# Attention units 4 to 7: from the weight tiles ahead of the first block to pool tiles between its products

## The chip, the cores and the metric

One core of one Trainium2 chip (trn2) runs the whole program. The metric is the device time of one execution in microseconds; the time of before is the median of three runs. In the views PE is TensorE's matmul stream, DVE is VectorE, ACT ScalarE, POOL GpSimd and SP SyncE, which issues all DMAs here.

## The reference

Three stages follow each other. Attention has four batches, eight heads, 576 tokens and a head dimension of 64, in float32; a gated MLP widens 512 to 1536, a second MLP widens 512 to 2048. The weights are float64.

```python
# attention: a mean over groups of four tokens, plus a window of +-3 tokens
q_d = q.reshape(B, H, Sd, 4, D).mean(axis=3)      # k_d, v_d likewise
out_d = softmax(scale * q_d @ k_d.T) @ v_d
out_up = np.repeat(out_d, 4, axis=2)
out_local = softmax(where(|i - j| < 4, scale * q @ k.T, -1e9)) @ v
x = (out_up + out_local)                          # then (2304, 512)
# gated MLP
g = x @ w_gate
x = (g * sigmoid(g) * (x @ w_val)) @ w_out
# second MLP
h = x @ w_in
out = (max(h, 0) + alpha * min(h, 0)) @ w_out2
```

## The kernel before, in words

**Blocks and steps.** The 2304 tokens form eight blocks of 288 (half a batch's sequence). For each block the first MLP runs twelve steps j, each over 128 of the 1536 hidden columns: `m_g` (12 products into g), `m_v` (12 into v) and, one step late, `m_y` (12 into y, which collects over the twelve steps). Float32 accuracy comes from splitting each operand into a high half and a rest: `mm3` makes three products of each (high by high, high by rest, rest by high). So a step is 36 products of 288 columns, a block 432. After g a Tanh on ACT (L512) and a multiplication on DVE (L513) follow, after v another on DVE (L519), then ph (the high half, ACT L522) and pl (the rest, POOL L523), which y needs.

**Weights.** A float64 weight tile of 512 KB (`raw`) is loaded by SP (L104, L106) and split on the chip by `w_split`, three a step (g, v, o). ACT makes a float32 from the upper words (L129). Then there are two forms. With a staging tile in one of three weight slots (`st_slots`: o10, g11, v11) ACT also fetches the top byte (L137) and DVE joins them in one instruction (L139). With a staging tile "st" of the pool, DVE joins them in two (L131, L132). `NEARLY` says from which step on the second form is used. At last ACT makes the high half (L142) and POOL the low half (L143). The split weights stay on the chip for all eight blocks, so loads and splits happen only in the first 143 us.

**Attention units.** A block needs four units of two heads each, unit n = 4 blk + hp, so units 0 to 3 feed block 0, units 4 to 7 block 1. A unit is `a_T` (k and q transposed), `a_QK` (scores on PE, L345 and L349; the mask, the maxima on DVE, the subtraction on POOL L371), `a_EXP` (ACT L388), `a_NRM` (sums on DVE, the scaling on POOL L408, then four transposes on DVE into a block-diagonal tile bd, L419), `a_PT` (transposes on PE, copied to pt) and `a_PV` (second products on PE, L446 and L450, then up on ACT L454, xf on DVE L455, xh on ACT L459, xl on POOL L460). xh and xl are the block's operand. The units of a batch's first half also sum v in groups of four on POOL (`a_vd`, L332 and L333): the tile vd has one buffer, so its next load waits until both instructions have read it. v's windows are copied within HBM by `stage(b)` (1.5 MB a batch) and then loaded as vw.

**Where the units' tiles lie.** With `NPRO = 8` units 0 to 7 work in weight tiles that no weight needs yet. `pslot` gives each tile a slot: the k tile of units 0 to 3 and the vd tile are used again as q and as scratch by units 4 to 7. From unit 8 on, units use single pool tiles (qn, qT, sm, pt, vw, xf). A weight that shares its slot with a unit's tile can be loaded only when that unit is through.

**What sets the order.** The tile framework's scheduler orders each engine's instructions; the code says where a unit stands: units 0 to 7 are written ahead of the products, later units by `at(position, ...)`, with 36 positions a block (three a step) and `run(position)` between `m_g`, `m_v` and `m_y`. Unit 8's scores stand at position 25 (`OFF`), later ones nine apart, second products eleven positions behind the scores. `prep1(j)` splits a step; `gP` holds POOL's part of the first splits back behind a stage of units 0 to 3. SP issues in order, with eight DMA semaphores in turn, so an issue also waits for the DMA eight places earlier.

Of the kernel before, what the change touches and what calls it, by code (L numbers as in the profile page):

```python
# [18 lines left out]

K = dict(kdP=0, qdP=0, dnP=2, ldn=9, lo='asvw0123', NPRO=8, c=5, a1=1, a2=0, OFF=25, oT=3, oE=3, oP=5, oV=11, vd1=2, vd2=1, pre=(1, 1, 0, 0), lo1=0, lo2=1, nst=3, nrm=0, sub=0, nrm1=0, sub1=0, qtA=0, ldw=1, xl1=0, ly=4, l2=3, st2=2, early=1, w2p=1, la=0, bdV=0, sp=9, s2=0, s3=0, gj=7, gs=1, vr=0, kc=0, gD=(0, 0, 0, 0, 0, 0), gP=(0, 2, 8, 8, 0, 0), gA=(0, 0, 0, 0, 0, 0))  # L20


@with_exitstack
def attn_moe_moe2_kernel(
# [13 lines left out]
    nc = tc.nc  # L38
# [18 lines left out]
    SW = LW + SD  # L57
    NBD, NVD, NVW, NSM, NST = 1, 1, 1, 1, 2
    scale = 1.0 / float(D) ** 0.5
# [99 lines left out]
    order = [f"{kind}{j}" for j in range(F1 - 8, F1) for kind in "gvo"]  # L159
    st_slots = order[5 * NP:][:K["nst"]]  # L160
    NEARLY = F1 - 2
    pslot = {(what, n): order[4 * i + n] for i, what in enumerate(("qv", "qs", "kn", "vd", "bd")) for n in range(NP)}
    for n in range(NP):
        pslot["qv", n + NP] = pslot["kn", n]
        pslot["qs", n + NP] = pslot["qs" if K["vr"] else "vd", n]
    NPRO = K["NPRO"]
# [70 lines left out]
    def a_load_w(n):  # L237

        b, half, hp, blk = coords(n)
        if n < NP:  # L240
            pbd[n] = at_(n, [128, 2, NW, 128], "bd")
            (nc.vector if K["bdV"] else nc.gpsimd).memset(pbd[n], 0.0)
# [149 lines left out]
    def a_NRM(n):  # L392
# [23 lines left out]
        d["bd"] = pbd[n % NP] if n < NPRO else bds[n % NBD]  # L416
        for i in range(NS):
# [70 lines left out]
    def gate(n, stage):  # L488

        bb = tc.nc.cur_bb.bb.instructions  # L490
        for key, eng in (("D", nc.vector), ("P", nc.gpsimd), ("A", nc.scalar)):
            gates[key, n, stage] = next(i for i in reversed(bb) if i.engine == eng.engine)

    def prep1(j):
        with ExitStack() as es:
            for key in "DPA":
                g = K["g" + key][j] if j < 6 else 0
                if g and (key, (g - 1) // 2, (g - 1) % 2) in gates:
                    es.enter_context(tc.issue_after(gates[key, (g - 1) // 2, (g - 1) % 2]))
            prep1_(j)  # L500
# [25 lines left out]
    def m_y(blk, j):  # L526
# [5 lines left out]
        if j == F1 - 1:  # L532
            for e in range(KD):
                if blk == NB1 - 1:
                    ys = side2.tile([128, 512], F32, tag="sy", name="sy", bufs=2)[:, :HB]
                elif e % 2:
                    continue
                else:
                    ys = hp_.tile([128, 2, HB], F32, tag="st", name="ys", bufs=NST)
                n = 1 if blk == NB1 - 1 else 2  # L540
                src = Y[e // 2][:, e % 2, :HB] if n == 1 else Y[e // 2][:, :, :HB]
                nc.scalar.copy(out=ys, in_=src)  # L542
                nc.sync.dma_start(
                    out=y1[e * 128:(e + n) * 128, blk * HB:(blk + 1) * HB].rearrange("(e p) t -> p e t", p=128),
                    in_=ys.unsqueeze(1) if n == 1 else ys)

# [83 lines left out]
    if True:  # L630
# [34 lines left out]
        def a_all(n, A):  # L665
# [13 lines left out]
            if K["vd1"] == 3:  # L679
                a_vd(n)  # L680
            a_PV(n, A)

        pc = [0]
# [7 lines left out]
        for n in range(NP):  # L691
            a_all(n, P[n])
        preps(K["pre"][1])
        pstack.close()
        pg2 = ctx.enter_context(tc.tile_pool(name="pg2", bufs=1, space=PSUM))
        GV[0] = pg2.tile([128, 512], F32, name="g")
        GV[1] = pg2.tile([128, 512], F32, name="v")
        for n in range(NP, NPRO):
            a_load(n)
            a_load_w(n)  # L700
        for n in range(NP, NPRO):
            if n == NP + 2:
                preps(K["pre"][2])
            a_all(n, P[n % NP % 3])
        preps(K["pre"][3])
        def load8():
            if B > 1:
                stage(1)
            a_load(NPRO)
            a_load_v(NPRO)  # L710
            a_load_w(NPRO)

        for j in range(4, F1 - 2):
            load1(j)
        with tc.issue_after(wdma[f"o{K['gj']}"]):
            load8()
        for b in range(2, B):
            if K["gs"] == 0:
                stage(b)
        nc.sync.dma_start(out=alpha_sb, in_=alpha.rearrange("(j p) -> p j", p=128))  # L720
# [38 lines left out]
        for i, (blk, j) in enumerate(fts):  # L759
# [9 lines left out]
            if blk == 0:  # L769
                while pc[0] <= min(j + K["early"], F1 - 1):  # L770
                    prep1(pc[0])
                    pc[0] += 1
                    if pc[0] == NEARLY:
                        load1(F1 - 2)
                        load1(F1 - 1)
                        if K["gs"]:
                            with tc.issue_after(wdma[f"o{F1 - 1}"]):
                                for b in range(2, B):
                                    stage(b)
            m_g(blk, j)  # L780
# [64 lines left out]
```

## Time and profile before

| what | before |
| --- | --- |
| median of three runs | 1017.37 us (1016.74 to 1018.96) |
| the profiled execution | 1017.97 us, span 1015.9 us, mean granted clock 0.995 |
| PE busy | 969.7 us (95%) |
| DVE, ACT, POOL busy | 478.9, 306.8, 383.5 us (47%, 30%, 38%) |
| HBM read, written | 67.12 MB, 15.73 MB |

The busy shares say that PE sets the time on the whole. They are means over stages: loads, splits and units 0 to 7 fill the first 150 us, the blocks with PE full follow. The table of stretches below tells them apart; its columns are the stretch, its length, the busy time and (in brackets) the instructions of PE, PEld (weight loads), DVE, ACT and POOL, the granted clock as a share of full speed, the DMA share and GB/s. In a timeline each line is one instruction (or a few alike): start, duration, engine, line, what it writes and reads, and in brackets the idle time ahead of it with what ended it.

### The profile page before, as it was taken

How to read it: one execution, taken by the hardware profiler on the slowest of the kernel's cores; microseconds unless marked ns; L12 is line 12 of the kernel's file. 1: busy time of each engine (PE TensorE's matmuls, PEld its weight loads, DVE VectorE, ACT ScalarE, POOL GpSimd, SP SyncE). 2: the span in 40 equal slices, each digit the busy share in tenths (PEclk: the TensorE clock that was granted, in tenths of full speed). 3: DMA queues.
4: the chain of work that ended last, by engine and by line, in shares of the span. 5: the costliest groups of instructions: out<-in, count | busy, mean ns of one | idle time of the engine just before them, and what ended most of it. 6: DMA issues, size and time to landing. Idle time of an engine off the chain costs nothing.

```text
span 1015.9 us, 19233 instructions
## 1 busy us (share of the span) xinstructions
PE 969.7 (95%) x7760; PEld 865.3 (85%) x7760; DVE 478.9 (47%) x1015; ACT 306.8 (30%) x690; POOL 383.5 (38%) x492
## 2 busy tenths in 40 slices
PE   5489789999999999999999999999999999999998
PEld 4379679999999999999999998888888888888897
DVE  5577864555444555444532769622222322322232
ACT  3869632222221322222323556312111101211111
POOL 5868763234322344222223435624223322322222
PEclk9999899999999999999999999999999999999999
DMA  8998741132111321110103883102000100100010
GB/s 202 290 315 283 184 93 27 35 73 59 38 46 21 76 50 41 40 26 18 43 9 116 282 254 122 42 1 63 22 0 21 52 1 1 42 11 1 0 43 22
DMA packets 135894, 77.81 MB, mean 77 GB/s; under 512 B 97406, under 2 KB 127102, under 8 KB 135038
## 3 DMA queue, kind: packets, MB, share of 16 engines
q1 hardware_dynamic: 135804, 76.58, 27.0%
q8 instruction: 60, 0.98, 0.4%
q14 instruction: 30, 0.25, 0.1%
HBM read 67.12 MB, written 15.73 MB: 82 GB/s over the span
## 4 chain that ended last, share of the span: by engine, by line
PE 82%; SPq 4%; DVE 4%; DMA 3%; POOL 3%; issue 2%; ACT 2%; POOLq 0%; DVEq 0%; ACTq 0%
PE y L610 7%; PE y L612 6%; PE y L611 6%; PE g L473 6%; PE v L474 6%; PE v L473 6%; PE v L475 6%; PE g L474 6%; PE g L475 6%; PE y L473 4%; PE y L475 4%; PE y L474 4%; PE h L473 3%; PE h L475 3%; PE h L474 3%
## 5 line engine op out<-in xcount | busy, mean ns | idle before, releaser
L598 POOL TENSOR_TENSOR gl<-t,gh 128x512 fp32r<-128x512 f32 (+1 forms) x80 | 97.0, 1214 | 250.9 <-ACT gh L597 244.4
L597 ACT CAST gh<-t 128x512 fp32r<-128x512 f32 (+1 forms) x80 | 46.2, 578 | 278.7 <-DVE t L594 239.2
L473 PE MATMUL g<-xh,w 128*128 128x288 f32 x384 | 117.4, 306 | 10.0 <-DVE u L513 4.4
L475 PE MATMUL g<-xh,w 128*128 128x288 f32 x384 | 115.1, 300 | 1.9 <-POOL w L143 1.8
L473 PE MATMUL v<-xh,w 128*128 128x288 f32 x384 | 116.0, 302 | 0.6 <-ACT w L142 0.4
L474 PE MATMUL v<-xl,w 128*128 128x288 f32 x384 | 115.3, 300 | 0.0
L474 PE MATMUL g<-xl,w 128*128 128x288 f32 x384 | 115.0, 300 | 0.0
L474 PE MATMUL y<-pl,w 128*128 128x288 f32 x384 | 113.8, 298 | 1.3 <-POOL pl L523 1.2
L475 PE MATMUL v<-xh,w 128*128 128x288 f32 x384 | 113.8, 296 | 0.6 <-POOL w L143 0.6
L610 PE MATMUL y<-w,gh 128*128 128x512 f32 x288 | 113.2, 393 | 1.0 <-ACT sy L542 1.0
L475 PE MATMUL y<-ph,w 128*128 128x288 f32 x384 | 113.0, 296 | 0.0
L611 PE MATMUL y<-w,gh 128*128 128x512 f32 x288 | 112.8, 392 | 0.0
L612 PE MATMUL y<-w,gl 128*128 128x512 f32 x288 | 112.0, 392 | 0.0
L513 DVE SCALAR_TENSOR_TENSOR u<-u,g 128x288 f32<-128x288 f32 x96 | 43.3, 451 | 144.1 <-ACT u L512 144.1
L473 PE MATMUL y<-ph,w 128*128 128x288 f32 x384 | 111.0, 301 | 0.2 <-ACT ph L522 0.2
L523 POOL TENSOR_TENSOR pl<-u,ph 128x288 fp32r<-128x288 f32 x96 | 79.8, 832 | 59.4 <-ACT ph L522 58.6
L143 POOL TENSOR_TENSOR w<-st,w 128x512 fp32r<-128x512 f32 x52 | 70.2, 1356 | 60.7 <-ACT w L142 60.5
L473 PEld LDWEIGHTS g<-xh,w 128*128 128x128 f32 x384 | 73.5, 191 | 12.9 <-DVE u L513 5.7
L592 DVE TENSOR_SCALAR t<-h,alpha 128x512 f32<-128x512 f32 (+1 forms) x40 | 27.9, 697 | 110.7 <-PE h L475 109.5
L512 ACT ACTIVATE u<-g 128x288 f32<-128x288 f32 x96 | 39.4, 410 | 122.8 <-PE g L475 121.3
L475 PEld LDWEIGHTS g<-xh,w 128*128 128x128 f32 x384 | 73.7, 192 | 2.7 <-POOL w L143 2.4
L473 PEld LDWEIGHTS v<-xh,w 128*128 128x128 f32 x384 | 72.8, 190 | 2.3 <-DVE u L519 1.0
(190 smaller groups left out, 2143.4 us busy)
## 6 DMA issues: line engine op xcount, KB each, us to landing
raw<-in_moe_w_out_dram SPq DMA_DIRECT2D x28, 512.0 KB
raw<-in_moe_w_in_dram SPq DMA_DIRECT2D x16, 512.0 KB
raw<-in_moe_w_gate_dram SPq DMA_DIRECT2D x12, 512.0 KB
raw<-in_moe_w_val_dram SPq DMA_DIRECT2D x12, 512.0 KB
vw<-vwin SPq DMA_DIRECT2D x48, 96.0 KB
out_dram<-os SPq DMA_DIRECT2D x18, 256.0 KB
sy<-y SPq DMA_DIRECT2D x16, 256.0 KB
y<-ys SPq DMA_DIRECT2D x14, 288.0 KB
```

Source lines behind the costliest of these rows:

```text
L143: eng.tensor_sub(w[:, 1], st, f32(w[:, 0]))
L473: nc.tensor.matmul(o, lhi, rhi, start=first, stop=False)
L474: nc.tensor.matmul(o, lhi, rlo, start=False, stop=False)
L475: nc.tensor.matmul(o, llo, rhi, start=False, stop=last)
L512: nc.scalar.activation(out=u, in_=GV[0][:, :HB], func=AF.Tanh, scale=0.5)
L513: nc.vector.scalar_tensor_tensor(out=u, in0=u, scalar=1.0, in1=GV[0][:, :HB], op0=ALU.add, op1=ALU.mult)
L523: nc.gpsimd.tensor_sub(pl, u, f32(ph))
L597: nc.scalar.copy(out=gh[:, :n], in_=t[:, :n])
L598: nc.gpsimd.tensor_sub(gl[:, :n], t[:, :n], f32(gh[:, :n]))
L610: nc.tensor.matmul(o, gh[:, ms], ohi, start=(j == 0), stop=False)
L611: nc.tensor.matmul(o, gh[:, ms], olo, start=False, stop=False)
L612: nc.tensor.matmul(o, gl[:, ms], ohi, start=False, stop=(j == F2 - 1))
```

## The change

Units 4 to 7 are no longer written ahead of the products. `NPRO` is 4: only units 0 to 3 use weight tiles, and units 4 to 7 take pool tiles and positions of their own: scores seven positions apart from position 1 on (`c = 7`), transposes six, second products seven positions behind the scores. Their q and k come by DVE transposes, not PE transposes. Unit 8 starts at position 30 instead of 25. The slots of units 0 to 3 are dealt out anew: k and vd tiles in the slots of steps 4 and 5 first. `NEARLY` goes from 10 to 8, so that the splits of steps 8 to 11 use the two-step form on DVE (twelve splits, not six), and `st` and the y copies have three buffers. Splits 1 to 3 are held behind unit 3 on DVE, POOL and ACT, not on POOL alone. The copy of y out of PSUM at a block's end is four copies and four DMAs of 288 columns, not two of 576. The windows of batch 1 are copied behind o of step 9, those of batches 2 and 3 at position 36 behind g and v of step 11. Lines of after stand three lines higher from 146 on, one line higher from about 500.

```diff
-K = dict(... NPRO=8, c=5, a1=1, a2=0, OFF=25, ... gj=7, ... gP=(0, 2, 8, 8, 0, 0), ...)
+K = dict(... NPRO=4, c=7, a1=1, a2=0, OFF=30, ... gj=9, ...)
-    NBD, NVD, NVW, NSM, NST = 1, 1, 1, 1, 2
+    NBD, NVD, NVW, NSM, NST = 1, 1, 1, 1, 3
-    NEARLY = F1 - 2
-    pslot = {... enumerate(("qv", "qs", "kn", "vd", "bd")) for n in range(NP)}
-    for n in range(NP):
-        pslot["qv", n + NP] = pslot["kn", n]
-        pslot["qs", n + NP] = pslot["qs" if K["vr"] else "vd", n]
+    NEARLY = F1 - 4
+    pslot = {... enumerate(("kn", "vd", "qv", "bd", "qs")) for n in range(NP)}
+    behind = {1: (NP - 1, 1), 2: (NP - 1, 2), 3: (NP - 1, 2)}
     def prep1(j):
         with ExitStack() as es:
-            for key in "DPA":
-                g = K["g" + key][j] if j < 6 else 0
-                if g and (key, (g - 1) // 2, (g - 1) % 2) in gates:
-                    es.enter_context(tc.issue_after(gates[key, (g - 1) // 2, (g - 1) % 2]))
+            if j in behind:
+                for key in "DPA":
+                    es.enter_context(tc.issue_after(gates[(key, *behind[j])]))
             prep1_(j)
@@ m_y
-                    ys = hp_.tile([128, 2, HB], F32, tag="st", name="ys", bufs=NST)
+                ys = pool.tile([128, 512], F32, tag=tag, name="ys", bufs=n)[:, :HB]
+                nc.scalar.copy(out=ys, in_=Y[e // 2][:, e % 2, :HB])
+                nc.sync.dma_start(out=y1[e * 128:(e + 1) * 128, blk * HB:(blk + 1) * HB], in_=ys)
@@ ahead of the blocks
-        for n in range(NP, NPRO):
-            a_load(n)
-            a_load_w(n)
-        for n in range(NP, NPRO):
-            a_all(n, P[n % NP % 3])
-        for j in range(4, F1 - 2):
+        a_load(NPRO)
+        a_load_w(NPRO)
+        for j in range(4, NEARLY + 2):
             load1(j)
-        with tc.issue_after(wdma[f"o{K['gj']}"]):
-            load8()
+        def stage_rest():
+            with tc.issue_after(wdma[f"g{F1 - 1}"]), tc.issue_after(wdma[f"v{F1 - 1}"]):
+                for b in range(2, B):
+                    stage(b)
+        at(36, stage_rest)
@@ first block, after the splits of step 7
                         load1(F1 - 2)
                         load1(F1 - 1)
-                        if K["gs"]:
-                            with tc.issue_after(wdma[f"o{F1 - 1}"]):
-                                for b in range(2, B):
-                                    stage(b)
+                        with tc.issue_after(wdma[f"o{NEARLY + 1}"]):
+                            stage(1)
```

On PE, at the end of block 0: y_70 is the accumulator of y, g that of the next step's gate; L345 and L342 are scores of an attention unit. Before, the last y product is followed by block 1's next step:

```order
L473 MATMUL y_70<-ph,w 128x288
L474 MATMUL y_70<-pl,w 128x288
L475 MATMUL y_70<-ph,w 128x288
L473 MATMUL g<-xh,w 128x288
L474 MATMUL g<-xl,w 128x288
L475 MATMUL g<-xh,w 128x288
```

and now, at the same place (L423 transposes and L443, L447 second products of unit 6, L342, L346 scores of unit 7):

```order
L472 MATMUL y_70<-ph,w 128x288
L423 MATMUL att<-ident,sm 72x72 x4
L443 MATMUL att<-pt,vs 64x72 x4
L447 MATMUL att<-bd_80,vw 64x96 x6
L342 MATMUL att<-kT,qT 32x32 x24
L346 MATMUL att<-kd,qd 72x144 x2
L470 MATMUL g<-xh,w 128x288
L470 MATMUL v<-xh,w 128x288
L471 MATMUL g<-xl,w 128x288
L472 MATMUL g<-xh,w 128x288
```

Two units' steps moved from ahead of block 0's products to behind its last one; six products stand between unit 7's scores and its transposes, and six more behind its second products.

On SP, before, the last weights stand among the loads of units 8 and 9 (L206 k and q, L235 vd, L248 vw):

```order
L104 DMA raw<-in_moe_w_out_dram 128x1024 x2
L257 DMA vwin<-in_v_dram 192x2048
L206 DMA kn<-in_k_dram 32x18x32 x4
L206 DMA qn<-in_q_dram 32x9x32 x4
L235 DMA vd<-in_v_dram 72x2x256
L106 DMA raw<-in_moe_w_val_dram 128x4x256
L106 DMA raw<-in_moe_w_gate_dram 128x4x256
L248 DMA vw<-vwin 128x3x64 x2
L206 DMA kn<-in_k_dram 32x18x32 x4
```

and now (L203 k and q, L232 vd, L245 vw, L254 the windows):

```order
L106 DMA raw<-in_moe_w_val_dram 128x4x256 x2
L104 DMA raw<-in_moe_w_out_dram 128x1024 x2
L106 DMA raw<-in_moe_w_gate_dram 128x4x256
L104 DMA raw<-in_moe_w_out_dram 128x1024
L254 DMA vwin<-in_v_dram 192x2048
L106 DMA raw<-in_moe_w_gate_dram 128x4x256
L106 DMA raw<-in_moe_w_val_dram 128x4x256
L203 DMA qn<-in_q_dram 32x9x32 x4
L245 DMA vw<-vwin 128x3x64 x2
L203 DMA kn<-in_k_dram 32x18x32 x4
L232 DMA vd<-in_v_dram 72x2x256
L104 DMA raw<-in_moe_w_out_dram 128x1024
```

The weights of steps 4 to 9 and g and v of step 10 moved ahead of units 5's to 7's q; only o10, g11, v11 and o11 stand among or behind them.

On POOL, before, behind the third last low half (L143), the sums of v (L332, L333) stand among the last splits:

```order
L332 TENSOR_TENSOR vd<-vd 72x2x128
L143 TENSOR_TENSOR w<-st,w 128x512
L333 TENSOR_TENSOR vs<-vd 72x128
L408 TENSOR_TENSOR sm<-sm,sr_82 128x2x96
L143 TENSOR_TENSOR w<-st,w 128x512
L332 TENSOR_TENSOR vd<-vd 72x2x128
```

and now, behind the last low half (L329, L330 sums of v; L368 subtraction, L405 scaling, L457 xl):

```order
L329 TENSOR_TENSOR vd<-vd 72x2x128
L330 TENSOR_TENSOR vs<-vd 72x128
L457 TENSOR_TENSOR xl<-xf,xh 128x288
L522 TENSOR_TENSOR pl<-u,ph 128x288
L329 TENSOR_TENSOR vd<-vd 72x2x128
L279 MEMSET qT 128x8
L282 MEMSET kT 128x3
L283 MEMSET kT 128x5
L330 TENSOR_TENSOR vs<-vd 72x128
L368 TENSOR_TENSOR sm<-sm,mx 128x2x96
L329 TENSOR_TENSOR vd<-vd 72x2x128
L405 TENSOR_TENSOR sm<-sm,sr_83 128x2x96
```

The sums of v for units 9 to 11 moved from among the last splits to between the POOL steps of units 6 and 7.

## Rows read from the trace of the kernel before

**Rows 1.** Table of stretches; columns as told above.

```profile
76.20:101.60 25.40, 25.37 (x250) 24.33 (x247) 19.30 (x35) 23.04 (x53) 21.97 (x22) 1.00 0.82 283
101.60:127.00 25.40, 19.75 (x215) 17.52 (x214) 22.79 (x38) 16.12 (x31) 19.69 (x21) 0.87 0.77 184
...
143.00:200.00 57.00, 56.88 (x586) 53.81 (x587) 26.99 (x72) 14.04 (x36) 19.08 (x32) 1.00 0.19 43
```

**Rows 2.** Timeline of PE, 48 to 149 us.

```profile
48.43 0.61 PE L473 MATMUL g<-xh,w 128*128 128x288 f32 x1 [3.20 <-DVE qs L455]
...
49.07 0.44 PE L475 MATMUL g<-xh,w 128*128 128x288 f32 x1
49.31 0.44 PE L473 MATMUL g<-xh,w 128*128 128x288 f32 x1
...
52.91 0.38 PE L473 MATMUL g<-xh,w 128*128 128x288 f32 x1
...
121.15 0.61 PE L475 MATMUL g<-xh,w 128*128 128x288 f32 x1 [1.83 <-POOL w L143]
...
148.72 0.29 PE L475 MATMUL y<-ph,w 128*128 128x288 f32 x1
148.85 0.29 PE L473 MATMUL g<-xh,w 128*128 128x288 f32 x1
```

**Rows 3.** Timeline of SP's DMA issues, weights alone, 80 to 123 us.

```profile
83.30 12.37 SPq L104 DMA_DIRECT2D raw<-in_moe_w_out_dram  x2
...
105.85 0.40 SPq L106 DMA_DIRECT2D raw<-in_moe_w_val_dram  x1
...
122.92 0.41 SPq L106 DMA_DIRECT2D raw<-in_moe_w_val_dram  x1
```

**Rows 4.** POOL by line, 48.43 to 143; L143 by stretch (DVE, POOL); the last one.

```profile
L143 POOL TENSOR_TENSOR w<-st,w 128x512 fp32r<-128x512 f32 x30 | 40.5, 1362 | 11.6 <-ACT w L142 11.4
L523 POOL TENSOR_TENSOR pl<-u,ph 128x288 fp32r<-128x288 f32 x11 | 10.3, 936 | 0.8 <-ACT ph L522 0.4 <-issue 0.2
...
25.40:60.40 35.00, 0.00 (x0) 16.34 (x12) 1.00 0.95 273
78.30:112.80 34.50, 0.00 (x0) 19.48 (x15) 1.00 0.79 247
...
141.37 1.27 POOL L143 TENSOR_TENSOR w<-st,w 128x512 fp32r<-128x512 f32 x1
```

**Rows 5.** DVE: the two-step form by line, 48.43 to 143, and three single instructions.

```profile
L131 DVE TENSOR_SCALAR st<-st 128x512 int32<-128x512 int32 x6 | 5.9, 995 | 0.0
...
96.79 0.42 DVE L131 TENSOR_SCALAR st<-st 128x512 int32<-128x512 int32 x1
97.24 1.83 DVE L132 SCALAR_TENSOR_TENSOR st<-raw,st 128x512 int32<-128x512 int32 x1
...
112.30 2.63 DVE L131 TENSOR_SCALAR st<-st 128x512 int32<-128x512 int32 x1
```

**Rows 6.** Timelines of PE, POOL and DVE, one unit in block 1.

```profile
172.53 0.62 PE L345 MATMUL att<-kT,qT 64*32 64x32 f32 x48
...
178.17 0.47 PE L446 MATMUL att<-pt,vs 72*64 72x72 f32 x8
...
177.11 0.51 POOL L408 TENSOR_TENSOR sm<-sm,sr 128x192 f32<-128x192 f32 x1 [1.58 <-DVE sr L401]
181.81 0.80 POOL L460 TENSOR_TENSOR xl<-xf,xh 128x288 fp32r<-128x288 f32 x1 [4.19 <-ACT xh L459]
...
179.26 1.52 DVE L419 STREAM_TRANSPOSE bd<-sm 32x192 f32<-32x192 f32 x4 [0.99 <-PE att L450]
```

**Rows 7.** Timeline of POOL, the sums of v.

```profile
143.24 0.74 POOL L332 TENSOR_TENSOR vd<-vd 72x256 f32<-72x256 f32 x1 [0.60 <-DMA vd<-in_v_dram]
...
147.65 0.73 POOL L332 TENSOR_TENSOR vd<-vd 72x256 f32<-72x256 f32 x1 [1.73 <-DMA vd<-in_v_dram]
...
151.52 0.73 POOL L332 TENSOR_TENSOR vd<-vd 72x256 f32<-72x256 f32 x1 [1.84 <-DMA vd<-in_v_dram]
```

More of the change, by code (lines that the diff above doesn't have):

```diff
@@ L17 @@
 DRAM = bass.MemoryType.DRAM
-K = dict(kdP=0, qdP=0, dnP=2, ldn=9, lo='asvw0123', NPRO=8, c=5, a1=1, a2=0, OFF=25, oT=3, oE=3, oP=5, oV=11, vd1=2, vd2=1, pre=(1, 1, 0, 0), lo1=0, lo2=1, nst=3, nrm=0, sub=0, nrm1=0, sub1=0, qtA=0, ldw=1, xl1=0, ly=4, l2=3, st2=2, early=1, w2p=1, la=0, bdV=0, sp=9, s2=0, s3=0, gj=7, gs=1, vr=0, kc=0, gD=(0, 0, 0, 0, 0, 0), gP=(0, 2, 8, 8, 0, 0), gA=(0, 0, 0, 0, 0, 0))
+K = dict(kdP=0, qdP=0, dnP=2, ldn=9, lo='asvw0123', NPRO=4, c=7, a1=1, a2=0, OFF=30, oT=3, oE=3, oP=5, oV=11, vd1=2, vd2=1, pre=(1, 1, 0, 0), lo1=0, lo2=1, nst=3, nrm=0, sub=0, nrm1=0, sub1=0, qtA=0, ldw=1, xl1=0, ly=4, l2=3, st2=2, early=1, w2p=1, la=0, bdV=0, sp=9, s2=0, s3=0, gj=9, gs=1, vr=0, kc=0)
 @with_exitstack
@@ L159, in attn_moe_moe2_kernel @@
     order = [f"{kind}{j}" for j in range(F1 - 8, F1) for kind in "gvo"]
-    st_slots = order[5 * NP:][:K["nst"]]
-    NEARLY = F1 - 2
-    pslot = {(what, n): order[4 * i + n] for i, what in enumerate(("qv", "qs", "kn", "vd", "bd")) for n in range(NP)}
-    for n in range(NP):
-        pslot["qv", n + NP] = pslot["kn", n]
-        pslot["qs", n + NP] = pslot["qs" if K["vr"] else "vd", n]
+    st_slots = order[5 * NP:][:3]
+    NEARLY = F1 - 4
+    pslot = {(what, n): order[4 * i + n] for i, what in enumerate(("kn", "vd", "qv", "bd", "qs")) for n in range(NP)}
     NPRO = K["NPRO"]
@@ L241, in a_load_w @@
             pbd[n] = at_(n, [128, 2, NW, 128], "bd")
-            (nc.vector if K["bdV"] else nc.gpsimd).memset(pbd[n], 0.0)
+            nc.gpsimd.memset(pbd[n], 0.0)
         if n >= NPRO:
@@ L415, in a_NRM @@
                                 in1=sr[:72, 6:8].unsqueeze(2).to_broadcast([72, 2, SD]), op=ALU.mult)
-        d["bd"] = pbd[n % NP] if n < NPRO else bds[n % NBD]
+        d["bd"] = pbd[n] if n < NPRO else bds[0]
         for i in range(NS):
@@ L533, in m_y @@
             for e in range(KD):
[L534 to L538, printed above, removed]
-                    ys = hp_.tile([128, 2, HB], F32, tag="st", name="ys", bufs=NST)
[L540 to L545, printed above, removed]
+                pool, tag, n = (side2, "sy", 2) if blk == NB1 - 1 else (hp_, "st", NST)
+                ys = pool.tile([128, 512], F32, tag=tag, name="ys", bufs=n)[:, :HB]
+                nc.scalar.copy(out=ys, in_=Y[e // 2][:, e % 2, :HB])
+                nc.sync.dma_start(out=y1[e * 128:(e + 1) * 128, blk * HB:(blk + 1) * HB], in_=ys)
     blocks2 = [512, 512, 512, 512, 256]
@@ L681, in a_all @@
             a_PV(n, A)
+            gate(n, 2)
         pc = [0]
@@ L692, in attn_moe_moe2_kernel @@
             a_all(n, P[n])
-        preps(K["pre"][1])
+        preps(1)
         pstack.close()
@@ L775, in attn_moe_moe2_kernel @@
                         load1(F1 - 1)
-                        if K["gs"]:
-                            with tc.issue_after(wdma[f"o{F1 - 1}"]):
-                                for b in range(2, B):
-                                    stage(b)
+                        with tc.issue_after(wdma[f"o{NEARLY + 1}"]):
+                            stage(1)
             m_g(blk, j)
```

10 lines of the change are left out of this document (removed).

## The prediction, made before the changed kernel ran

> **What bounds the kernel now.** I read the table of stretches first. From 143 us on TensorE (PE) is busy 56.88 of 57.00 us [rows 1], so whatever the change moves behind that point is worth nothing; only what lies ahead can be won. There the same table shows two kinds of stretch: 76.20 to 101.60 with PE full (25.37 of 25.40), and 101.60 to 127.00 with PE at 19.75 and a granted clock of 0.87 [rows 1].
>
> The timeline of PE prices the loss. The first product of the block starts at 48.43. Products follow each other by 0.24 us after an idle stretch (49.07, 49.31, until 52.91) and by 0.13 at the end of block 0 (148.72, 148.85) [rows 2]: the two levels, 1.2 and 2.4 GHz. The product at 148.85 is the first behind block 0's last one. By then 468 products have run (432 of block 0, 36 of block 1). 468 x 0.133 = 62.2 us. Units 4 to 7 take some 2.1 us of PE each (estimate: the scores are 0.62 us [rows 6], the transposes, the second products and the rest about 1.5), 8.5 us, and units 8 to 10 some 5. That makes 76 of the 100.4 us between 48.43 and 148.85. About **24 us are lost**, and that is the most that this change can bring.
>
> Who ends the waits? In 101.60 to 127.00 they end on a weight half: the product at 121.15 waited 1.83 us for POOL's low half (L143) and restarted at the slow level [rows 2]. The weights were late because they were loaded late: SP issues no weight between o's pair at 83.30 and a v at 105.85; the last v comes at 122.92 [rows 3]. The tiles of these loads held units 4 to 7 or the staging of the splits. POOL ends its last low half at 141.37 + 1.27 = 142.64 [rows 4], and block 0 ends 148.85 - 142.64 = **6.2 us** behind it.
>
> **What the change removes.** The weight tiles are free of units 4 to 7, so no load waits for them; the order of SP shows the weights of steps 4 to 9 and g and v of step 10 ahead of every piece of units 5 to 7. The eight steps behind the first four (24 splits) can then run as densely as the engines allow. Let p be the time of the last low half, 142.64 now.
>
> *p, from the engine sums.* In before the first twelve low halves are done by 60.4 [rows 4]; units 4 to 7's transposes and copies no longer stand among them, I take 59. From there POOL has 24 halves x 1.36 = 32.7, ten pl x 0.94 = 9.4 [rows 4], one xl 0.8, the subtraction and the scaling of units 4 and 5 (four of 0.51 [rows 6], 2.0) and two sums of v with as long again for what follows them (0.74 [rows 7], 3.0): 47.9 us. With no idle time p = 107; at POOL's share of the densest stretch, 21.97/25.40 = 0.865, p = 59 + 55.4 = 114. In that stretch ACT was fuller (23.04/25.40 = 0.91 [rows 1]), and twelve of the 24 splits lose one of ACT's three passes. I therefore take the middle, not the end that the old share gives: **p = 111**, bounds 106 (the durations hold waits that vanish when fewer operations meet) and 116.
>
> *The splits' new mix.* With 12 instead of 6 splits in two DVE steps (L131 + L132 instead of L139), six are added. By the shortest row L131 is 0.42 us (96.79), and the row at 112.30 is 2.63 us, its POOL neighbour being busy with low halves; the mean of the six is 0.995 [rows 5]. Six more cost DVE 6 x 0.42 = 2.5 to 6 x 2.63 = 15.8 us, by the mean 6.0; I take the mean, since these six meet the same POOL load. DVE has room for that (19.30 of 25.40 us busy in the dense stretch), so it goes into p's upper bound only.
>
> The Trainium skill, page "SBUF — State Buffer", section "Who interferes with whom", states that DVE and GpSimd share one port pair as an exclusive lock held for a whole instruction, that tensor_scalar in its two-port mode takes it and that an operation with two SBUF inputs contends with GpSimd's reads. By that rule the trace agrees at 97.24 (L132 1.83 us beside a row of three low halves), and the added L131 would lengthen POOL's sum instead of filling DVE's gaps: p would be 111 + 6 = 117. This is the page's reason for the second rival.
>
> **What the change moves, and where it costs.** Units 4 and 5 now run inside block 0 and cost PE the same 2.1 us each as before. Units 6 and 7 do not fit: by the order of PE, unit 6's scores stand behind the last but one y step, its transposes behind block 0's last product, and unit 7's scores behind unit 6's second products; only 24 products of block 1 (four k-slices of g and v) lie beside all this, and the last six of them need unit 7's output. So behind p stands a **serial chain** that the trace of before hid.
>
> Its price comes from a unit in the full part of block 1: scores at 172.53, the scaling on POOL ends 177.62, plus 1.52 for the four transposes: 6.6 us from scores to bd. From second products at 178.17 to the end of xl at 182.61 it is 4.4, with DVE away for 1.52 on other transposes: 2.9 for second products, xf, xh and xl [rows 6]. The next unit's scores need xf only (xl 0.8 and xh about 0.4 less): 1.7. So one unit from scores to the next one's scores is 6.6 + 1.7 = 8.3 us if nothing is in the way. In the way are, on POOL, the vd sums of units 9 to 11, which stand in the order between the subtraction, the scaling and xl of units 6 and 7, and each waits for a load into one single buffer: sums at 143.24, 147.65 and 151.52 are 4.4 and 3.9 us apart [rows 7]. Three stand in unit 6's chain and two in unit 7's, so a unit takes 8.3 us (they are hidden) to 3 x 3.9 = 11.7 (they set the pace). I take 10.0, the middle, since chain and loads run side by side and the later of the two ends each step.
>
> The walk: unit 6's scores at p + 4 (the last v step's eviction, pl, then twelve y products at 0.133), block 0 ends at p + 6.2 as now, unit 7's scores at p + 14, its xl ends at p + 14 + 6.6 + 2.9 + 1.8 for vd = p + 25.3, and the last six products, at the slow level, at **p + 26.7**. The restart at that level costs another 2.0 us (48.43 to 52.91 at 0.24 instead of 0.133), so the same work in full flow stands at p + 28.7. Bounds: 8.3 a unit gives p + 25.2, 11.7 gives p + 32.
>
> At the same point of work (456 products, units to 7 and unit 8's scores) before stood at 148.85 - 12 x 0.133 - about 3.7 for units 8 to 10 = 143.5. With p = 111 after stands there at 139.7: a gain of **3.8 us** of 24, 1014.2 against the profiled run's 1017.97; that run lies 0.6 above the median 1017.37, so I say **1014**, the upper side of 1013.6 to 1014.2.
>
> **Edits with no price.** The four y copies of 288 columns in place of two of 576 add two instructions on ACT and two DMAs once a block, beside products (PE is full there at 56.88 of 57.00); if uncovered, about 0.5 us a block, seven blocks, 3.5 us. Units from 8 on start five positions later and keep nine between them; the last one of a block ends some 37 products (4.9 us) ahead of its use. That covers the 2.9 us from second products to xl [rows 6]; without it each of six boundaries costs the difference. The windows of batches 2 and 3 now load at 110 to 120 us instead of 55, beside qn, kn and vd of units 6 to 11: 3 MB at 283 GB/s [rows 1] is 11 us of the queue, and can push one vd back by that; it is in the second rival.
>
> **The rivals.**
>
> *More is won (1004 to 1010).* p = 106 and units at 8.3 us: 143.5 - 106 - 25.2 = 12.3 us gained, 1005. For it: before's DVE and POOL idle a quarter and an eighth even in the dense stretch. Against it: the chain behind block 0 has too few products beside it in the order to vanish. Chance 0.15.
>
> *The new chain costs more than the loads give (slower).* The place is POOL between block 0's last pl and xl of unit 7; the price is 11.7 us a unit, or the page's lock with p = 117. It decides from p + chain = 145.5 on (2 us behind before). With p = 115 and 11.7 a unit: 147, a loss of 3.5, 1021. For it: vd round trips of 3.9 to 4.4 us and the 3 MB of windows just ahead of them. Against: the loads of the windows go out once. Chance 0.24.
>
> *Nothing comes of it.* The weights come earlier, the chain eats exactly that: p of 113 to 117 with units at 10 gives a gain of 1.8 to a loss of 2.2 us. The same if the change doesn't do what it says, that is if the loads go out early but DVE and POOL split at the old 2.3 us each (15 halves in 78.3 to 112.8 [rows 4]: 24 x 2.3 = 55, p = 114). Chance 0.23.
>
> **How the numbers follow.** The forecast, faster by 2 to 7 us, 0.38; more 0.15; none 0.23; slower 0.24. 0.2% is 2.0 us, about what a measurement here can tell from no change. Faster 0.53, same 0.23, slower 0.24. The range takes the forecast with its bounds and most of both rivals: 1004 to 1021.
>
> **What would show it.** In the profile after: weight loads of steps 8 to 11 issued before 85 us but for the last three; the last L143 between 106 and 116; PE with its waits not inside block 0 but in one stretch of some 20 us behind its last product, ended by unit 6's and 7's bd, pt and xl, at the granted clock's lower level; no idle time on PE from 150 on. Wrong would be: PE waits inside block 0 at the old places (p above 120), POOL waiting for vd through the whole stretch (slower), or units 6 and 7 hidden (more is won); or new waits of PE at each block's start.

## The result: slower by 1.5%

The changed kernel takes 1032.32 us (median of four, 1031.43 to 1033.21) against 1017.06 (1016.09 to 1018.96): ratio 1.0148, 95% interval 1.0130 to 1.0166. The profiled execution has a span of 1029.7 us against 1015.9, so 13.8 us are to be found. The range of the prediction ended at 1021.

The stretches of the changed kernel, with the columns of [rows 1]:

```profile
44.94:60.00 15.06, 12.18 (x94) 11.06 (x95) 10.66 (x15) 12.52 (x25) 12.38 (x14) 0.50 1.01 315
...
76.20:101.60 25.40, 16.94 (x109) 16.03 (x109) 23.37 (x24) 17.16 (x35) 22.30 (x19) 0.89 0.78 256
101.60:127.00 25.40, 25.40 (x245) 24.50 (x244) 20.93 (x41) 13.69 (x33) 21.70 (x23) 0.98 0.61 181
127.00:152.40 25.40, 12.95 (x197) 9.86 (x203) 11.69 (x32) 6.82 (x24) 8.27 (x20) 0.62 0.45 99
152.40:180.00 27.60, 26.30 (x274) 24.21 (x275) 16.17 (x41) 6.53 (x18) 9.15 (x15) 0.85 0.16 35
180.00:200.00 20.00, 20.00 (x253) 18.90 (x252) 11.62 (x33) 5.21 (x14) 5.69 (x10) 1.00 0.14 26
```

From 165 us on PE is full, as it is in the kernel before from 143. The hole is 127.00 to 152.40: PE busy 12.95 of 25.40 us at a granted clock of 0.62, with DVE, ACT and POOL each less than half busy. No engine is short of time there; they wait for each other. In 76.20 to 101.60 PE, full before [rows 1], is busy 16.94, while DVE has 23.37. The count of products run shows what that stretch cost: by 76.20 us it is 148 with unit 4 done, in the kernel before 84 with units 4 to 6 done; by 101.60 it is 255 with unit 4, before 251 with units 4 to 7. At 0.133 us a product and 2.8 us a unit (below) that is, as an estimate, a lead of 2.9 us that became a lag of 7.9.

PE behind the last splits (L342 scores, L423 transposes of pt, L443 second products; the bracket names what ended the idle time):

```profile
127.34 0.62 PE L342 MATMUL att<-kT,qT 64*32 64x32 f32 x48
...
131.05 0.29 PE L472 MATMUL y<-ph,w 128*128 128x288 f32 x1
...
135.43 0.76 PE L423 MATMUL att<-ident,sm 72*72 72x72 f32 x4 [4.08 <-ACT sm L409]
136.68 0.75 PE L443 MATMUL att<-pt,vs 72*64 72x72 f32 x8 [0.48 <-ACT pt L426]
...
139.21 0.76 PE L342 MATMUL att<-kT,qT 64*32 64x32 f32 x48 [0.82 <-DVE xf L452]
...
148.51 0.76 PE L423 MATMUL att<-ident,sm 72*72 72x72 f32 x4 [4.71 <-ACT sm L409]
...
152.29 0.76 PE L342 MATMUL att<-kT,qT 64*32 64x32 f32 x48 [0.82 <-DVE xf L452]
...
157.08 0.61 PE L470 MATMUL g<-xh,w 128*128 128x288 f32 x1 [0.51 <-DVE u L512]
```

131.05 is block 0's last product; in the kernel before that is 148.72 [rows 2], so block 0 ends **17.7 us earlier**. Block 1 is measured from the first copy of y behind block 0 to the first behind block 1, in the kernel before

```profile
148.38 1.30 ACT L542 COPY ys<-y 128x576 f32<-128x576 f32 x2 [0.42 <-PE y L475]
...
213.49 0.63 ACT L542 COPY ys<-y 128x576 f32<-128x576 f32 x1
```

and in the changed kernel

```profile
130.72 1.12 ACT L535 COPY ys<-y 128x288 f32<-128x288 f32 x3 [4.29 <-PE y L472]
...
226.84 1.03 ACT L535 COPY ys<-y 128x288 f32<-128x288 f32 x3
```

It takes 96.1 us against 65.1, **31.0 us more**, and ends 13.3 us later. Three parts make that up. PE waits 13.7 us between 131 and 158 (8.8 for the softmax of units 6 and 7, 1.8 for xl, 1.6 for xf, 1.5 for the rest). Work that the kernel before had done by the end of its block 0 is done in block 1 now: 24 products, 3.2 us, and 2.7 units' scores, four units' transposes and three units' second products, about three units at 2.8 us, 8.4 (a later block takes 68.7 us, of which 432 x 0.133 = 57.5 are products, so four units take 11.2), together 11.6. The rest, 31.0 - 13.7 - 11.6 = 5.7 us, is put down to the lower clock, products 0.24 apart. Another unit's scores are still owed at the end of block 1. So at the end of block 0 the changed kernel owed 3.2 us of products and some 3.5 units, 9.7 us: of the 17.7 us only about 5 were won; the rest was put off.

### The profile page after: what moved, and what is told of

Read it like the earlier page. It is cut to its first block, busy times and chain, and to the rows that moved or that the text cites. A ratio compares the mean times of both kernels' runs of the same rounds, so it can differ in the third digit from the quotient of the medians.

```text
span 1029.7 us, 19276 instructions
## 1 busy us (share of the span) xinstructions
PE 975.9 (95%) x7748; PEld 871.4 (85%) x7748; DVE 502.4 (49%) x1021; ACT 307.8 (30%) x698; POOL 387.1 (38%) x492
## 4 chain that ended last, share of the span: by engine, by line
PE 83%; DVE 4%; DMA 4%; SPq 3%; ACT 2%; issue 2%; POOL 2%; POOLq 0%; ACTq 0%; DVEq 0%
PE y L601 6%; PE y L603 6%; PE y L602 6%; PE v L470 6%; PE g L470 6%; PE g L471 6%; PE g L472 6%; PE v L471 6%; PE v L472 6%; PE y L470 4%; PE y L471 4%; PE y L472 4%; PE h L470 3%; PE h L472 3%; PE h L471 3%
## 5 line engine op out<-in xcount | busy, mean ns | idle before, releaser
L470 PE MATMUL g<-xh,w 128*128 128x288 f32 x384 | 120.4, 314 | 10.4 <-DVE u L512 7.9
L470 PE MATMUL v<-xh,w 128*128 128x288 f32 x384 | 118.4, 308 | 2.8 <-DVE u L518 2.8
L471 PE MATMUL g<-xl,w 128*128 128x288 f32 x384 | 117.6, 306 | 3.2 <-POOL xl L457 3.2
L512 DVE SCALAR_TENSOR_TENSOR u<-u,g 128x288 f32<-128x288 f32 x96 | 43.1, 449 | 158.6 <-ACT u L511 155.3
L472 PE MATMUL g<-xh,w 128*128 128x288 f32 x384 | 116.6, 304 | 0.0
L472 PE MATMUL v<-xh,w 128*128 128x288 f32 x384 | 114.8, 299 | 0.0
L143 POOL TENSOR_TENSOR w<-st,w 128x512 fp32r<-128x512 f32 x52 | 73.0, 1414 | 36.3 <-ACT w L142 36.0
L471 PEld LDWEIGHTS g<-xl,w 128*128 128x128 f32 x384 | 74.6, 194 | 5.6 <-POOL xl L457 4.2
```

What stands on the lines that cost most here:

```text
L143: eng.tensor_sub(w[:, 1], st, f32(w[:, 0]))
L470: nc.tensor.matmul(o, lhi, rhi, start=first, stop=False)
L471: nc.tensor.matmul(o, lhi, rlo, start=False, stop=False)
L472: nc.tensor.matmul(o, llo, rhi, start=False, stop=last)
L512: nc.vector.scalar_tensor_tensor(out=u, in0=u, scalar=1.0, in1=GV[0][:, :HB], op0=ALU.add, op1=ALU.mult)
```

## The experiments

All times are medians; "p" is the end of the last low half, "scores apart" the distance from one unit's scores to the next. The kernel before measured between 1016.3 and 1017.7 us beside them, the changed kernel 1032.3. The theory at first was the second rival: POOL's order with the sums of v, and the port.

**Taking one part of the change back, or moving one thing out of the stretch.** e1 and e9 put `tc.issue_after(...)` behind unit 7:

```diff
     def a_vd(n):                       # e1, units 9 to 11
+        with tc.issue_after(gates["P", 7, 2]): ...
     def a_T(n, A):                     # e9, these two as well
+        with tc.issue_after(gates["D", 7, 2]):
             nc.vector.transpose(out=kT[:, 3:S + 3], in_=d["kn"]); nc.vector.reduce_sum(kd, ...)
```

> The changed kernel, with the sums of v for units 9 to 11 (their POOL additions, and so the loads that refill the single vd buffer) issued behind unit 7's xl. Behind block 0 of the changed kernel the scores of units 6, 7 and 8 stand 11.9 and 13.1 us apart (127.34, 139.21, 152.29), and POOL's subtraction for unit 7 waits 2.59 us for a load of vd while its input was ready 3 us before. Theory vd (POOL's order with the sums of v sets the pace there): the scores come 9 to 10 us apart, block 1 ends 6 to 9 us earlier, 1023 to 1026 us. Rival (the units' own chain through single tiles sets it, the sums only fill it): within 2 us of 1032.

> The changed kernel, with the sums of v (POOL) and the preparation of k (two DVE instructions, 0.73 us each) for units 9 to 11 both held behind unit 7. With the sums of v alone held back (e1) unit 8's scores came 10.4 instead of 13.1 us behind unit 7's, unit 7's still 11.8 behind unit 6's, and between scores and the maximum DVE spent 1.5 us on another unit's k. Theory (work of units 9 to 11, put between the steps of units 6 to 8 by the schedule, sets their pace together): 9 to 10 us from scores to scores, another 2 to 4 us less than e1, 1026 to 1028. Rival (what is left is the chain itself, on PE at its lower clock, with the y copies on ACT): within 1.5 us of e1's 1030.3, since k then comes later for units 9 to 11.

e1 1030.3 us, e9 1029.9, both in the range of their rival. Scores in e9 (L356; L342 above):

```profile
128.60 0.62 PE L356 MATMUL att<-kT,qT 64*32 64x32 f32 x48
...
137.62 0.76 PE L356 MATMUL att<-kT,qT 64*32 64x32 f32 x48 [0.82 <-DVE xf L466]
...
147.02 0.76 PE L356 MATMUL att<-kT,qT 64*32 64x32 f32 x48 [0.82 <-DVE xf L466]
...
153.39 0.61 PE L484 MATMUL g<-xh,w 128*128 128x288 f32 x1 [3.19 <-DVE u L526]
```

9.0 and 9.4 us apart instead of 11.9 and 13.1: v and k of units 9 to 11, put between the steps of units 6 to 8, did set the pace (the theory of e9 holds for the pace, not for the time). But the time falls by 2.4 us only: that work has to be done behind, and there PE waits again (3.19 us for u at 153.39, 1.45 at 174.26), so that block 1 shrinks from 96.1 to 93.2 alone.

e2 puts q ahead:

```diff
-        for j in range(4, NEARLY + 2):
+        for j in range(4, 6):
             load1(j)
+        # behind unit 5's q: steps 6, 7; behind unit 6's q: steps 8, 9
+            with tc.issue_after(hu[n]["last"]):
```

> The changed kernel, with the weight loads of steps 6 and 7 held behind unit 5's q load, and those of steps 8 and 9 behind unit 6's. In the changed kernel unit 4's q tile is free at 50.75 us, but unit 5's q is issued at 79.23, behind 19 weight loads, and unit 5's scores stand behind product 295 of block 0. Theory load order (units 5 to 7 are late because q stands behind the weights in SP's queue): unit 5's scores move to about product 144, unit 6's to 259, two units fewer behind block 0, 12 to 18 us less idle PE there, 1014 to 1020 us. Rival (the engines are full with splits, so units moved into block 0 push the splits, and the last low half, back by as much): 1026 to 1032.

1025.2 us, between the two ranges. Unit 5's scores move from 107.51 to 77.35, unit 6's from 127.34 to 97.39:

```profile
77.35 0.62 PE L342 MATMUL att<-kT,qT 64*32 64x32 f32 x48
...
97.39 0.62 PE L342 MATMUL att<-kT,qT 64*32 64x32 f32 x48
```

Block 1 takes 87.4 us instead of 96.1 and block 0 ends 1.0 later. So units 5 and 6 were late because of their loads' place; unit 7's scores still come at 132.28, behind block 0. In the changed kernel's SP timeline q of unit 5 stands behind the weights:

```profile
77.58 1.56 SPq L106 DMA_DIRECT2D raw<-in_moe_w_val_dram  x1
79.23 8.59 SPq L203 DMA_DIRECT2D qn<-in_q_dram  x4
...
95.00 0.36 SPq L104 DMA_DIRECT2D raw<-in_moe_w_out_dram  x1
...
98.96 0.39 SPq L106 DMA_DIRECT2D raw<-in_moe_w_gate_dram  x1
...
108.80 0.40 SPq L106 DMA_DIRECT2D raw<-in_moe_w_val_dram  x1
109.24 2.04 SPq L254 DMA_DIRECT2D vwin<-in_v_dram  x3
```

e3 (`NEARLY = F1 - 2`), e4 (`issue_after` for POOL alone in `prep1`) and e10 (`issue_after(wdma["o9"])` for the windows, position 6):

> The changed kernel, with the two-step split on DVE from step 10 on (six splits, as before the change) instead of from step 8 (twelve). Theory port (DVE's operations with two inputs or in its fast mode and POOL's subtractions exclude each other; the sum of their shortest durations fills 60 to 122 us): six splits cost 0.68 instead of 0.41 + 0.67 us of it, the last low half comes 2.4 us (shortest rows) to 6 us (means 1.17 against 2.20) earlier than 121.9, and the time falls to 1026 to 1030. Rival (ACT's extra pass for the top byte, 0.67 us each, takes as much): the last low half within 1 us, 1031 to 1033; the units' order may move by itself.

> The changed kernel, with the splits of steps 1 to 3 held back on POOL alone, as before the change, not on DVE, POOL and ACT. In the changed kernel ten low halves are done by 60 us, in the kernel before twelve. Theory early splits: the first product no later than 45 us plus 1, twelve low halves by 60, the last one 2 to 4 us earlier than 121.9, 1028 to 1030. Rival (the end of the splits is set by the two engines' sum and not by their start): within 1.5 us of 1032.

> The changed kernel, with the windows of v for batches 2 and 3 issued behind o of step 9 instead of behind g and v of step 11. In the changed kernel they are issued at 109.24 to 124.83 us between k, q and vd of units 6, 7, 9 and 10; late windows alone, in the kernel before, made block 1 4.5 us longer. Theory (the windows hold up the loads that units 6 to 8 and the sums of v need): block 1 shrinks from 96.1 by 3 to 5 us, 1027 to 1030. Rival (they only fill a queue that is ahead anyway, or hold up v of step 11 as much): 1031 to 1034.

e3 1033.8 us with p = 128.7: both its theory and its rival miss. Fewer two-step splits do not bring p forward here, but the scheduler also moved units 5 and 6 among the splits (scores at 96.83 and 114.46), so the price of the form is not separated. e4 1032.5, p = 122.1 and twelve low halves at 60.2 instead of 63.4: its rival holds, and the gates cost nothing in the end. e10 1030.9, between the two ranges: block 1 takes 89.4, 6.7 less, but p = 129.9, 8 later.

**One part of the change alone in the kernel before.** e7 (`NEARLY = F1 - 4`), e8 (windows at position 36), e6:

```diff
-K = dict(... NPRO=8, ...)
+K = dict(... NPRO=6, ...)
-        at(0 if NPRO == NP else OFF - 7, lambda: a_pre(NPRO))
+        at(0, lambda: a_pre(NPRO))
```

> The kernel before, with units 6 and 7 alone moved to pool tiles and positions in block 0 (16 products of a step earlier or later as the scheduler places them); units 4 and 5 stay ahead in the weight tiles, splits, gates, y copies and window loads as before. In its order unit 6's scores stand at product 108 of block 0 and unit 7's at 230, its second products at 276, so nothing of them is left behind block 0. Theory (the loss of the change lies in the units left behind block 0, not in moving units as such): no idle stretch behind block 0, at the slow clock or otherwise; with half the weight tiles free sooner, 1008 to 1016 us. Rival (units among the splits cost the splits as much as the tiles give, whatever their number): 1016 to 1022.

> The kernel before, with one part of the change alone: the two-step split from step 8 on (twelve instead of six), the staging tiles freed two steps sooner. Theory port: six more joins cost DVE and POOL's shared time 6 x 0.4 us = 2.4, but g of step 11 and o of step 10 can load earlier than 115.25 and 121.13, where the last splits starved: the last low half moves from 142.6 to 138 to 141, 1013 to 1016 us. Rival (the added two-step joins hold POOL, as one L131 of 2.63 us beside a low half suggests): later by 3 to 6, 1019 to 1023.

> The kernel before, with one part of the change alone: the windows of v for batches 2 and 3 (3 MB within HBM) issued at position 36 behind g and v of step 11, not at 55 us among the weights of steps 4 and 5. Theory (loads bind the splits at 60 to 78 us, where POOL has two low halves in 18 us): step 4's weights come up to 8 us earlier, the last low half by less, since the last tiles wait for units 6 and 7: 1011 to 1016 us. Rival (the last splits wait for tiles and not for the queue): within 2 us of 1017; and if the late windows block the loads of units 9 to 11, 1018 to 1021.

e6 1024.1 us: no hole behind block 0 (block 1 takes 66.9), and yet 7.8 us slower, with p at 148.2 instead of 142.6; its rival holds, and goes past its end. e7 1019.2 (ratio 1.0025, 1.0014 to 1.0036), p = 143.7: the time of its rival, though p comes 1.1 us later and not 3 to 6. e8 1019.9 (1.0028, 1.0011 to 1.0045; single runs from 1015.0 to 1022.9): p = 139.5, 3.1 earlier, as its theory has it, but block 1 takes 69.6 instead of 65.1, with the windows now among the loads of units 9 to 11. Each of these parts alone costs a little.

**Low halves of o on DVE** (`lo1=1`): e5 in the changed kernel, e12 in the kernel before; e15 o and g (`lo1=2`), e16 e12 with e7.

> The changed kernel, with the low halves of the o weights (one split in three of the first MLP) subtracted on DVE (about 0.68 us, like its other two-input operations) instead of POOL (shortest 1.27 us). Theory port (DVE and POOL exclude each other while a low half and a joining instruction meet, and their shortest durations together fill 60 to 122 us): eight low halves there cost 0.68 instead of 1.27 us of the shared time, the last low half comes about 4.7 us earlier than 121.9, the time falls by 3 to 5 us, 1027 to 1029. Rival (each engine's own sum binds, DVE at 92% of 76 to 102 us being the fuller): DVE gets 5.4 us more, the last low half comes 3 to 5 us later, 1035 to 1037.

> The kernel before, with the low halves of o on DVE, as e5 did for the changed kernel. Theory port: in its dense stretch (78 to 113 us, 15 low halves in 34.5 us) five of them cost 0.68 instead of 1.27 us of DVE's and POOL's shared time: the last low half 2 to 4 us earlier than 142.6, 1013 to 1015 us. Rival (the last splits of the kernel before wait for weight tiles that units 6 and 7 and the staging hold, not for the engines): within 2 us of 1016.5.

> The kernel before, with the low halves of o and of g on DVE (e12 had o alone: 1015.6, the last low half at 138.8 instead of 142.6). Theory port (time that DVE and POOL share binds): another 2 to 3 us earlier, 1012 to 1015. Rival (DVE fills up): 1016 to 1020.

> The kernel before, with the low halves of o on DVE (e12) and the two-step split from step 8 on (e7, alone 2.9 us slower). Theory (e7's price was shared time, which e12 frees): the staging tiles free sooner and the time is e12's or better, 1012 to 1015.5. Rival (the two add: six more two-step joins cost 3 us whatever POOL does): 1018 to 1019.

e5 1027.5 us (1022.1 to 1028.9), 4.8 less, in the port theory's range but not by its path: p = 120.6, 1.3 earlier instead of 4.7, and most is won behind block 0, where block 1 takes 91.3 with unit 6's scores 3.9 us earlier. DVE's joining instructions there lose their waits: L139 0.96 us in the mean instead of 1.17, L131 0.74 instead of 1.21. **e12 beats both kernels**, by little: 1015.6 (ratio 0.9981, 0.9970 to 0.9993), p = 138.8; p moves as its theory has it, the time lies in the rival's range. e15 1016.5 (0.9988, 0.9976 to 0.9999), p = 137.7, the rival's time. e16 1025.2, p = 149.6: past both of its ranges.

**All four measures together** (e2, e9, e5, windows behind o9):

> The changed kernel with q of units 5 and 6 ahead of the weights (e2), k and v of units 9 to 11 behind unit 7, low halves of o on DVE (e5), windows of batches 2 and 3 behind o of step 9. In its order unit 6's scores stand at product 323, unit 7's at 410, its second products at 450, so about one unit's chain is left behind block 0 instead of three. Theory (the loss is the units left behind block 0): block 1 takes 72 to 78 us instead of 96, block 0 ends at 130 to 136, 1008 to 1015 us, better than both kernels. Rival (units among the splits push the last split back by what they give): block 0 ends past 138, 1017 to 1024.

1024.4 us. Unit 6's and 7's scores come at 104.6 and 127.9, p is 126.4, block 0 ends at 134.0, block 1 takes 85.7. Theory and rival both miss: PE still waits 9.4 us behind block 0, 4.78 of it in one piece for DVE's u.

**Leaving units 5 to 7 out.** `a_QK`, `a_EXP`, `a_NRM`, `a_PT` return at once for them, and `a_PV` copies xh and xl of block 0.

> The changed kernel without units 5 to 7 (scores, softmax and second products left out, block 1's operand for them copied from block 0's; their loads and q transposes stay). Theory (their chain behind block 0 is the loss): with PE's own work for them (3 x about 2.1 us) some 30 us go: 998 to 1005 us, the last low half within 2 us of 121.9 or up to 5 earlier if unit 5's steps made the gap at step 10. Rival (the stretch behind block 0 has other causes, as v's sums, the windows, y's copies): 1012 or more.

> The kernel before without units 5 to 7, in the same way. Their slots come free sooner and PE is spared 6 to 9 us. Theory (ahead of the products they cost little more than PE's work and some weight tiles): 1004 to 1011 us, so their price is 6 to 13 us here against about 30 in the changed kernel. Rival (they are what makes the last weights late: the last low half at 142.6 moves to 125): 996 to 1002, their price the same as in the changed kernel.

Changed kernel 1017.3 us, kernel before 1013.3. So units 5 to 7 cost **15.0 us in the changed kernel and 4.0 before**: 11 of the 15 us of the change are theirs. The other 4 are there without them; loads, windows, splits and unit 4 were not separated. In time, the changed kernel lies in the rival's range (1012 or more) and not in the theory's; the kernel before lies above both of its ranges. The place is the theory's all the same: the hole behind block 0 is gone, and block 1 takes 70.2 us instead of 96.1.

```profile
101.60:127.00 25.40, 20.41 (x131) 19.95 (x131) 21.18 (x32) 10.59 (x20) 19.62 (x20) 0.88 0.75 192
127.00:152.40 25.40, 23.86 (x280) 22.53 (x279) 16.02 (x43) 7.01 (x19) 11.45 (x21) 1.00 0.62 155
```

Of these 26 us some 18 are left at the end of block 1, since block 0 ends 8.2 us later (PE is busy 20.41 us in 101.60 to 127.00, where it had 25.40), and 15 at the end of the program. And the loss of 76 to 102 us stays without the units: 245 products by 101.60, where the changed kernel has 255. The last low half without them:

```profile
123.01 1.28 POOL L143 TENSOR_TENSOR w<-st,w 128x512 fp32r<-128x512 f32 x1 [0.20 <-ACT w L142]
```

It ends at 124.3, against 121.9 with them:

```profile
119.39 2.53 POOL L143 TENSOR_TENSOR w<-st,w 128x512 fp32r<-128x512 f32 x2
```

The units do not push the last split back; the splits take that long without them.

**Windows in SP's pause**, with e12: behind o of step 9 or of step 8.

> The kernel before, with the low halves of o on DVE (e12, 1015.6) and the windows of batches 2 and 3 behind o of step 9, in SP's pause at 83 to 95 us. Theory (the windows hold up step 4's weights early, and the loads of units 9 to 11 late; in the pause they hold up nothing): step 4's splits end by 76 instead of 80.3 us, the last one 2 to 4 us earlier than 138.8, block 1 stays at 65 us: 1011 to 1014. Rival (the last splits wait for staging tiles, whatever comes first): within 1.5 us of 1015.6.

> As e17, with the windows behind o of step 8 (behind g, v and o of step 9 in its order). Theory: as e17, 1011 to 1014, at most 1 us apart from it. Rival: within 1.5 us of 1015.6; above 1017 if the windows now hold up unit 8's loads.

1017.1 and 1016.7 us (1.0004, 0.9986 to 1.0022, and 1.0002, 0.9991 to 1.0012). Step 4's splits end at 76.0 and 76.6 instead of 80.3, the last at 138.6 and 139.7: no gain, as the rival has it (e17 lies at the edge of its 1.5 us). The start of the splits is not what sets their end here.

## Why the prediction was wrong

**Right:** that the later blocks have nothing to give or lose (block 2 takes 68.7 us now and 68.8 before, so the four y copies and the later positions cost nothing there); that only three of the last weights are loaded late (behind unit 5's q the trace has an o, a g and a v, not four loads); that units 6 and 7 stand behind block 0 in a serial chain at the lower clock (granted clock 0.55 from 131.30 to 152.40), with the sums of v in POOL's order. That was priced as the second rival, with the right place, at 3.5 us; 15 were measured. Wrong was that nothing behind 143 us can be lost: five of PE's waits, 7.3 us, lie there, up to 157.08.

**The two terms that failed**, in the prediction's own sum: p came 10.9 us later than 111, and the chain from p to the last product before full flow took 7.5 us longer (34.2, from 121.92 to 156.13, where the walk had 26.7). Together that is 18.4 us; from the forecast for the profiled run, 1014.2, to its 1031.87 it is 17.7.

**First mis-sized term: p = 111, bounds 106 and 116; measured 121.9.** The sum started at 59; twelve low halves were done at 63.4. The engine sum took POOL's durations and put the six added two-step joins into the upper bound only, because DVE had room. The rows of DVE in the changed kernel, 44 to 122 us, by line:

```profile
L139 DVE SCALAR_TENSOR_TENSOR st<-st 128x512 int32<-128x512 int32 x18 | 20.8, 1166 | 6.2 <-ACT st L137 6.1
L131 DVE TENSOR_SCALAR st<-st 128x512 int32<-128x512 int32 x12 | 14.5, 1210 | 0.0
L132 DVE SCALAR_TENSOR_TENSOR st<-raw,st 128x512 int32<-128x512 int32 x12 | 11.8, 986 | 0.2
```

and one of them, with what stands behind it on DVE and then on PE:

```profile
78.15 4.83 DVE L131 TENSOR_SCALAR st<-st 128x512 int32<-128x512 int32 x1
82.90 0.44 DVE L518 SCALAR_TENSOR_TENSOR u<-u,v 128x288 f32<-128x288 f32 x1
```

```profile
83.49 0.37 PE L470 MATMUL v<-xh,w 128*128 128x288 f32 x1 [2.77 <-DVE u L518]
...
97.94 0.61 PE L470 MATMUL g<-xh,w 128*128 128x288 f32 x1 [4.43 <-DVE u L512]
```

POOL beside that L131, from 77.77 to 82.69 without a pause (L330 and L457 are a sum of v and an xl):

```profile
77.77 1.30 POOL L143 TENSOR_TENSOR w<-st,w 128x512 fp32r<-128x512 f32 x1
79.02 0.46 POOL L330 TENSOR_TENSOR vs<-vd 72x128 f32<-72x128 f32 x1
79.44 1.29 POOL L143 TENSOR_TENSOR w<-st,w 128x512 fp32r<-128x512 f32 x1
80.68 0.79 POOL L457 TENSOR_TENSOR xl<-xf,xh 128x288 fp32r<-128x288 f32 x1
81.43 1.26 POOL L143 TENSOR_TENSOR w<-st,w 128x512 fp32r<-128x512 f32 x1
83.88 1.33 POOL L522 TENSOR_TENSOR pl<-u,ph 128x288 fp32r<-128x288 f32 x1 [1.19 <-ACT ph L521]
```

The L131 ends at 82.98, 0.29 us behind POOL's last instruction of that row.

L131's mean is 1.21 us, where [rows 5] had 0.995 and 0.42 for the shortest. Against the shortest rows (0.41, 0.67, and 0.68 for L139) the three lines took 9.6 + 3.8 + 8.7 = 22 us more, against 11 us for the same lines before; that this was time spent beside POOL is an estimate. DVE works in order, so the waiting instruction also holds up u (L512, L518), for which PE waits: 2.77 us at 83.49 and 4.43 at 97.94, where L512 starts at 97.45 though ACT's part of u was done at 93.29. The Trainium skill, page "SBUF — State Buffer", section "Who interferes with whom", states an exclusive lock on the port pair that DVE and GpSimd share. These rows agree with it; the prediction's sentence on it had p at 117.

**The path to block 0's end was wrong too.** The prediction let block 0 end 6.2 us behind p, as PE's waits before ended on weight halves (5.0 us on L142 and L143 in block 0). In the changed kernel no wait of PE in block 0 ends on one: 9.3 us are waits for u, the last of them ends at 97.94, 24 us ahead of p, and PE then runs without a pause to block 0's end, 9.1 us behind p. By the trace it is DVE, nearly full from 76 to 102 us, that cost block 0 its lead, and p itself was not waited for.

That the lock alone makes p is **not shown**: with the low halves of o on DVE the same excess is 13.6 us, and p is 120.6; without units 5 to 7 it is 124.3, with the gates on POOL alone 122.1. The three weight loads behind unit 5's q (95.00 to 108.80) feed the last splits; nothing that was run moved p ahead of 120, and what sets it is left open between the chain of splits through three staging tiles and those loads. Whatever is the cause, a sum of one engine's durations was the wrong way to it: POOL, DVE and ACT hand each split on in order, and none was full for the whole stretch.

**Second mis-sized term: the chain, 10.0 us a unit; measured 11.9 and 13.1.** The bounds were 8.3 and 11.7. Missing were the preparation of another unit's k on DVE (0.73 twice a unit, between scores and the last maximum; with it and the sums of v held back, e9, the scores stand 9.0 and 9.4 apart), the sums' second wait (`vs` of a pair of heads is one tile, so POOL's L330 for unit 10 waits for unit 6's second products), and the y copies on ACT (three buffers for four copies: the last waits 1.86 us for a DMA, with unit 6's L409 behind it). On POOL:

```profile
137.59 0.45 POOL L330 TENSOR_TENSOR vs<-vd 72x128 f32<-72x128 f32 x1 [2.30 <-PE att L443]
...
145.54 0.72 POOL L329 TENSOR_TENSOR vd<-vd 72x256 f32<-72x256 f32 x1 [2.59 <-DMA vd<-in_v_dram]
146.22 0.50 POOL L368 TENSOR_TENSOR sm<-sm,mx 128x192 f32<-128x192 f32 x1
```

Unit 7's subtraction (146.22) had its input at 143.02 and stood behind a sum of v that waited for its load. Five such waits stand between unit 6's scores and unit 7's xl, 1.54 to 2.91 us each, where [rows 7] had 0.60 to 1.84. How the missing time divides among the three was not separated.

**A step that was missing:** why units 6 and 7 stand behind block 0. The prediction read their place in the order and took it as given. For unit 6 it comes from unit 5's q behind the weight loads on SP; with q of units 5 and 6 ahead the kernel takes 7 us less (e2).

**The third rival** of the prediction, that the chain eats what the loads give, had the two sides right and their sizes wrong: on the same footing of work block 0 gave about 5 us, and the waits and the lower clock behind it took 13.7 + 5.7 = 19.4.

## What to carry to other kernels

Before work is moved out from ahead of a busy engine, look in the order at whether it lands beside other work or behind it: units 5 to 7 cost 11 us more here than ahead of the products, although DVE, ACT and POOL were each less than half busy behind block 0. Check that the event whose time you add up is one that the busy engine waits for. Count, for the moved step, its loads' place in the DMA queue, and each single buffer that another unit's work wants in between. And take waits beside a partner engine as part of a duration: a mean of six rows grew by a fifth when twelve had to share.

## What the runs showed of the hardware that was not expected

One DVE instruction (L131), 0.43 us in the median of the program, took 4.83 us beside five POOL instructions in a row, with no wait recorded ahead of it; the time is in its own duration. In the changed kernel the first products ran 0.24 us apart from 44.94 until 61.6, at a granted clock of 0.50, interrupted by waits of 1.42 and 1.45 us; in the kernel before from 48.43 to 52.91 without a break [rows 2], a stretch for which the granted clock reads 1.00 all the same. The earlier start was worth nothing by 61.6 us: 48 products and one unit's scores had run, in the kernel before 37 products and three units' scores, about the same work; the lower clock (48 x 0.107 = 5.1 us) and the waits had taken it.
